# Query weights of a decode layer: eight loads of sixteen rows, eight partitions apart, in place of one load of 128 rows

## The chip, the cores and the metric

The kernel runs on one core of one Trainium2 chip. The metric is the device time of one execution in microseconds (us). One execution was also recorded by the hardware profiler; its lines are quoted as "the profile", and its events in order of time as "the trace". Engines are PE (TensorE matmul), PEld (its weight load), DVE (VectorE), ACT (ScalarE), POOL (GpSimd) and SP (SyncE, which here only issues DMAs); a name with q, such as SPq, is the sequencer of that engine.

## What is computed

One decode step of a transformer layer for a batch of 4, with a cache of 8192 positions for 32 heads of 128, in bf16:

```
h  = x + attention(layernorm(x), k_cache, v_cache, wq, wo)
       q = layernorm(x) @ wq                 # [4, 512] @ [512, 4096]
       p = softmax(q . k_cache / sqrt(128))  # for each batch and head
       o = (p . v_cache) @ wo                # [4, 4096] @ [4096, 512]
h2 = h + (sigmoid(n @ w_gate) * (n @ w_up)) @ w_down   # n = layernorm(h), 512 -> 1792 -> 512
```

## The kernel before

The 128 pairs of batch and head are worked in 32 units of four heads (NU = 32, HU = 4). The cache of a unit is 8 MB for K and 8 MB for V, and each is brought in by one DMA over 128 partitions, 64 KB a partition. The SBUF tile KV has three slots of that size: K goes to slots 0 and 1 in turn, V to slot 2 (the last V to slot 0). The weights borrow slots: the query weights wq (4 MB, 32 KB a partition) are in slot 2 at the start, before V0 takes it; wo, the gate and up weights follow the last K in slot 1, and the down weights follow in slot 2.

The program is a list of instructions for each engine, written out by the Python code with waits on semaphores (`prog.emit`, `prog.dma`); loops repeat two units at a time. No scheduler moves anything: each engine works in the order of its list.

SP's list holds all large loads on one queue. It begins with wq (L532), then the 64 cache loads (L541) in the order K0, K1, V0, K2, V1, K3, and so on, then wo, gate, up and down (L546 to L557). K0 and K1 wait for nothing. V0 waits for `t_qp`, the end of the q projection on PE, since it overwrites wq. A later K waits until DVE is through with the K two units before it (`t_kd`, L361), a later V until PE is through with the V one unit before it (`t_vd`, L419). A DMA raises its semaphore by 16 when it has landed; `t_wq = prog.token("wq", 16)` (L228) is the count that the readers of wq wait for.

The start on the other engines: the rows x are loaded by ACT's queue (L235), normalized by DVE and ACT (L273 to L277), turned by PE (L283). Then PE makes q in two groups of 16 matmuls (L301), which wait for wq, DVE turns the result (L308, L309) and builds the window Lq of the first query (L328). Per unit, DVE transposes K in chunks of 1024 words (L335), PE multiplies them (L344), DVE and ACT do the softmax (L362 to L375), PE multiplies with V (L405). After the last unit come the output projection (L475), a second layernorm and the gated feed-forward part (L501 to L530).

The destination and the source of the load that the diff touches:

```
reg(2, 0, NC * H * DH)                        # slot 2 of KV: 128 partitions x 16384 bf16
A_wq.rearrange("(p c) f -> p (c f)", p=128)   # 128 rows of 32 KB, contiguous in DRAM
```

Of the kernel before, what the change touches and what calls it, by code (L numbers as in the profile page):

```python
# [118 lines left out]
def bass_sequential_preLN__mha_block_cached__glu_gated_glu__decode_kernel(  # L119
# [13 lines left out]
    _, H, S, DH = A_k_cache.shape  # L133
    F = B_w_gate.shape[1]
    assert DH == 128 and H == 32 and D == 512 and F % 128 == 0 and B == 4 and S == 8192
    NC = D // 128
# [17 lines left out]
    prog = _Prog({"p2d": "dve", "d2d": "dve", "a2d": "dve", "d2p": "pe", "a2p": "pe",  # L154
                  "d2a": "act", "p2a": "act",
                  "k0": "dve", "k1": "dve", "v2": "pe"})
    emit = prog.emit

    with ExitStack() as es:
# [40 lines left out]
        def reg(slot, off, size):  # L200
            return KV[:, slot * SLOT + off:slot * SLOT + off + size]
# [23 lines left out]
        order = [("k", 0)] + [x for u in range(1, NU) for x in (("k", u), ("v", u - 1))] + [("v", NU - 1)]  # L225
        slots = {(x, u): (0 if u == NU - 1 else 2) if x == "v" else u % 2 for x, u in order}
        toks = {x: prog.token(x[0] + str(slots[x]), 16) for x in order}
        t_wq = prog.token("wq", 16)  # L228
        t_wo = prog.token("wo", 16)
        t_wg = prog.token("wg", 16)  # L230
        t_wu = [prog.token(f"wu{i}", 16) for i in range(len(WUC) - 1)]
# [293 lines left out]
        for t in range(NFT):  # L525
            if t == 0:
# [2 lines left out]
        t_o = [emit("dve", lambda e: e.tensor_copy(o_sb[:, 0:HD], bank[DN][0:B, 0:HD]), [t_d]),  # L529
               emit("act", lambda e: e.activation(o_sb[:, HD:D], bank[DN][32:32 + B, 0:HD], ACT.Copy), [t_d])]  # L530

        prog.dma("sp", "wq", lambda e: e.dma_start(reg(2, 0, NC * H * DH), A_wq.rearrange("(p c) f -> p (c f)", p=128)),  # L532
                 tok=t_wq)
        for n, (x, u) in enumerate(order):
            w = t_qp if n == 2 else None
            if n >= 3:
# [5 lines left out]
                     tok=toks[x, u])  # L542
# [49 lines left out]
```

## Time and profile before

| | |
|---|---|
| time, median of 3 runs | 1276.99 us (1276.86 to 1277.5) |
| the profiled execution, its time | 1276.65 us |
| its span in the profile | 1275.4 us |
| bytes read from DRAM | 550.77 MB, 432 GB/s over the span |
| mean granted TensorE clock | 0.823 |

The span runs from the first to the last recorded instruction; the time of the execution has 1.25 us around it. Three groups of instructions hold most of the busy time of the compute engines (columns: line, engine, operation, output and input tiles, shapes and count, then busy us and mean ns of one, then the idle time of the engine just before them and what ended most of it):

```profile
L335 DVE STREAM_TRANSPOSE kT<-KV 128x1024 f32<-128x1024 f32 x512 | 615.3, 1233 | 298.1 <-DMA KV<-in_A_k_cache_dram 237.2
L344 PE MATMUL PS<-kT,Lq 128*128 128x512 bf16 x2048 | 587.9, 419 | 315.5 <-DVE kT L335 298.5
L405 PE MATMUL PS<-KV,PTz 128*16 128x512 bf16 x2048 | 117.0, 381 | 0.3 <-DMA KV<-in_A_v_cache_dram 0.3
```

How to read it: a row of idle time names the releaser that ended it, here the K loads for DVE. A queue row of the DMA section gives packets, MB, and the time of its packets as a share of 16 engines' span. A row of DMA issues gives the median time from issue to landing, which includes what lay ahead in the queue.

### The profile page before, as it was taken

To read this page: it belongs to the slowest core of one execution; us is meant where nothing else is said; L and a number is where in the kernel's file an instruction comes from. 1 tells how busy PE (TensorE), PEld (TensorE's weight loads), DVE (VectorE), ACT (ScalarE), POOL (GpSimd) and SP (SyncE) were. 2 spreads that over 40 slices of the span, in tenths; PEclk is the share of its full clock that TensorE was granted. 3 is DMA by queue.
4 is the path that set the end of the run, shared out by engine and by line. 5 is a ranking of instruction groups with operands and counts; after the bars stand their busy time and mean duration, and the time that the engine had idled before them with its cause. 6 is when DMAs were issued, how large, how long until landed. Compare 5 with 4: busy or idle time off the path is not lost.

```text
span 1275.4 us, 14122 instructions
## 1 busy us (share of the span) xinstructions
PE 799.2 (63%) x4636; PEld 328.3 (26%) x4636; DVE 763.3 (60%) x917; ACT 58.9 (5%) x114; POOL 5.7 (0%) x22
## 2 busy tenths in 40 slices
PE   1676765557755557655567655567655576555677
PEld 0232222222222223222222222222222232222233
DVE  1876665556665557665567655566655566655571
ACT  2000000000000000000000000000000000000001
POOL 1000000000000000000000000000000000000000
PEclk9988877778877788777788877888777888777888
DMA  9999999999999999999999999999999999999998
GB/s 419 436 426 430 428 448 436 430 430 428 450 434 430 430 428 450 434 430 430 428 450 434 430 430 428 452 432 430 430 430 450 434 430 428 432 448 434 430 428 371
DMA packets 10388, 550.83 MB, mean 432 GB/s; under 512 B 1160, under 2 KB 1424, under 8 KB 1552
## 3 DMA queue, kind: packets, MB, share of 16 engines
q1 hardware_dynamic: 10368, 550.77, 99.7%
q8 instruction: 2, 0.03, 0.0%
q14 instruction: 2, 0.02, 0.0%
q10 hardware_dynamic: 16, 0.01, 0.0%
HBM read 550.77 MB, written 0.00 MB: 432 GB/s over the span
## 4 chain that ended last, share of the span: by engine, by line
DMA 41%; PE 13%; DVE 9%; issue 1%; ACT 1%; another core or an unknown queue 1%; SPq 0%; DVEq 0%
DMA KV<-in_A_k_cache_dram 39%; PE PS L344 10%; DVE kT L335 9%; PE PS L405 3%; DMA KV<-in_B_w_down_dram 3%; ACT kT L410 1%; PE PS L415 0%; SPq L541 0%; DVE PTz L375 0%; PE PS L521 0%; DVE KV L529 0%; SPq L557 0%; DVEq L112 0%
## 5 line engine op out<-in xcount | busy, mean ns | idle before, releaser
L335 DVE STREAM_TRANSPOSE kT<-KV 128x1024 f32<-128x1024 f32 x512 | 615.3, 1233 | 298.1 <-DMA KV<-in_A_k_cache_dram 237.2
L344 PE MATMUL PS<-kT,Lq 128*128 128x512 bf16 x2048 | 587.9, 419 | 315.5 <-DVE kT L335 298.5
L344 PEld LDWEIGHTS PS<-kT,Lq 128*128 x2048 | 210.1, 103 | 693.7 <-issue 620.7
L375 DVE STREAM_TRANSPOSE PTz<-E_sb 32x512 bf16<-32x512 bf16 x128 | 89.9, 703 | 129.1 <-PE PS L415 125.4
L405 PE MATMUL PS<-KV,PTz 128*16 128x512 bf16 x2048 | 117.0, 381 | 0.3 <-DMA KV<-in_A_v_cache_dram 0.3
L379 PE MATMUL PS<-part,headw 128*128 128x2 f32 x64 | 18.8, 363 | 100.5 <-DVE PTz L375 100.5
L369 ACT ACTIVATE E_sb<-PS,negm 128x512 bf16<-128x512 f32 x32 | 22.0, 687 | 1138.7 <-DVE negm L367 1138.7
L405 PEld LDWEIGHTS PS<-KV,PTz 128*16 128x16 bf16 x2048 | 58.8, 111 | 56.7 <-issue 13.2
L415 PE MATMUL PS<-lane,kT 128*128 128x4 f32 x256 | 33.6, 255 | 31.0 <-ACT kT L410 31.0
L362 DVE TENSOR_REDUCE part<-PS 128x1 f32<-128x512 f32 x32 | 22.1, 691 | 38.8 <-PE PS L344 38.8
L415 PEld LDWEIGHTS PS<-lane,kT 128*128 128x128 f32 x256 | 31.0, 191 | 46.2 <-issue 44.9
L379 PEld LDWEIGHTS PS<-part,headw 128*128 128x128 f32 x64 | 16.0, 310 | 103.7 <-DVE PTz L375 103.7
L322 PE MATMUL PS<-Lq,headw 128*128 128x512 bf16 x32 | 18.7, 585 | 10.8 <-issue 9.5
L410 ACT ACTIVATE kT<-PS,rsb 128x512 f32<-128x512 f32 x32 | 22.0, 687 | 61.2 <-PE PS L405 61.2
L388 PE MATMUL PS<-Lq 128*128 128x512 bf16 x44 | 13.2, 467 | 0.2 <-issue 0.2
L328 DVE TENSOR_TENSOR Lq<-q_all,mask 128x32 bf16<-128x32 bf16 x32 | 9.6, 300 | 0.0
L454 DVE TENSOR_TENSOR kT<-PS,mask 128x512 bf16<-128x512 f32 x1 | 0.7, 690 | 12.9 <-PE PS L415 12.9
L367 DVE STREAM_TRANSPOSE negm<-mxr 128x32 f32<-128x32 f32 x32 | 6.8, 212 | 1.1
L364 DVE STREAM_TRANSPOSE turn<-part 128x32 f32<-128x32 f32 x32 | 6.8, 212 | 1.1
L301 PE MATMUL PS<-KV,kT 128*4 128x512 bf16 x32 | 3.6, 627 | 5.4 <-DMA KV<-in_A_wq_dram 5.4
L388 PEld LDWEIGHTS PS<-Lq 128*128 128x128 bf16 x44 | 4.8, 115 | 8.1 <-issue 5.4
L396 DVE RECIPROCAL rsb<-PS 128x1 f32<-128x1 f32 x32 | 6.4, 199 | 0.7 <-PE PS L379 0.7
(70 smaller groups left out, 59.5 us busy)
## 6 DMA issues: line engine op xcount, KB each, us to landing
KV<-in_A_wq_dram SPq DMA_DIRECT2D x1, 4096.0 KB, 12.5
KV<-in_A_wo_dram SPq DMA_DIRECT2D x1, 4096.0 KB, 27.8
KV<-in_B_w_gate_dram SPq DMA_DIRECT2D x1, 1792.0 KB, 31.7
KV<-in_B_w_up_dram SPq DMA_DIRECT2D x1, 1792.0 KB, 35.5
KV<-in_B_w_down_dram SPq DMA_DIRECT2D x1, 1024.0 KB, 32.6
KV<-in_A_k_cache_dram SPq DMA_DIRECT2D x32, 49.6
KV<-in_A_v_cache_dram SPq DMA_DIRECT2D x32, 30.7
KV<-in_B_w_down_dram SPq DMA_DIRECT2D x1, 512.0 KB, 33.5
```

The costliest lines, as they stand in the source:

```text
L322: emit("pe", lambda e: e.matmul(bank[bk], headb, zeros, start=True, stop=False, skip_group_check=True), waits, incs=0)
L328: t_lq[u] = emit("dve", lambda e, ix: e.tensor_tensor(dst, bass.AP(raw(q_all), at(ix, 0) * (4 * TU) + 4 * (u - TU * t), [[NU * 4, 128], [1 ...
L335: t_tr[u, c] = emit("dve", lambda e: e.transpose(kT[:, (c % 2) * TW:(c % 2 + 1) * TW], KVw[:, o:o + TW]), w, ch="d2p")
L344: ins = e.matmul(bank[SBK], bass.AP(raw(Lq), ix[-1] * 2 + (128 * t + c % 2), [[528, 128], [1, 128]]), rhs, start=False, stop=False, skip_g ...
L362: a = emit("dve", lambda e: e.tensor_reduce(part[:, 0:1], bank[SBK], AX.X, ALU.max), [t_sc[u, NT - 1], t_pool], ch="d2d")
L369: t_exp[u] = emit("act", lambda e: e.activation(E_sb[:, :], bank[SBK], ACT.Exp, bias=negm[:, 0:1], scale=SCALE, accum_out=part[:, 1:2]), [ ...
L375: return [e.transpose(PTz[32 * q:32 * (q + 1), :].rearrange("p (r q c) -> p r q c", r=4, q=4)[:, :, q, :], E_sb[32 * q:32 * (q + 1), :].re ...
L379: t_sum[u] = emit("pe", lambda e: e.matmul(bank[QB[1]][:, 0:2], headw[:, :], part[:, 0:2], start=True, stop=True), [t_ptz[u], t_selc], ch= ...
L388: emit("pe", lambda e: [e.matmul(bank[XS], Lq[:, 0:128], Lq[:, 0:512], start=True, stop=True) for _ in range(n)][-1], [t_ps0, t_lq[NU - 1] ...
L405: made.append(e.matmul(PS[32 * j:32 * j + 16, ob:ob + 512], lhsT, KV[:, slot * SLOT + 512 * k:slot * SLOT + 512 * (k + 1)], start=(k < 4), ...
L410: t_ocp[u] = emit("act", lambda e: e.activation(O_sb, bank[OBK], ACT.Copy, scale=rsb[:, 0:1]), [t_pv[u], t_rs[u]], ch="a2p")
L415: ins = e.matmul(bass.AP(raw(PS), at(ix, 0) * 4 + (512 * EX + 4 * (u - t)), [[4096, 128], [1, 4]]), O_sb[:, 128 * q:128 * (q + 1)], lane[: ...
```

## The change

The one load of wq becomes eight. Load r takes rows r, r + 8, r + 16, ..., r + 120 of the source into the same partitions of slot 2, so that sixteen rows of 32 KB move with each load; together the eight write the same bytes to the same places. All eight raise the same semaphore, and `t_wq` is its count after all of them. They are issued one after the other from SP's list, ahead of K0.

```
-        t_wq = prog.token("wq", 16)
+        t_wq = prog.token("wq", 8 * 16)
...
-        prog.dma("sp", "wq", lambda e: e.dma_start(reg(2, 0, NC * H * DH), A_wq.rearrange("(p c) f -> p (c f)", p=128)),
-                 tok=t_wq)
+        wq_src = A_wq.rearrange("(p c) f -> p (c f)", p=128)
+        for r in range(8):
+            prog.dma("sp", "wq", lambda e, r=r: e.dma_start(reg(2, 0, NC * H * DH)[r:128:8, :], wq_src[r:128:8, :]), tok=t_wq)
```

SP's list at the start of the program, before (each row: line, what is issued, tiles and shape, repetitions, semaphores waited for; s_pe is the end of the q projection, s_d2x that of a K, s_p2x that of a V):

```order
L532 DMA KV<-in_A_wq_dram 128x16384 [waits barrier_Pool_Activation_PE_DVE_SP_release]
L541 DMA KV<-in_A_k_cache_dram 128x32768 x2
L541 DMA KV<-in_A_v_cache_dram 128x32768 [waits s_pe]
L541 DMA KV<-in_A_k_cache_dram 128x32768 [waits s_d2x]
L541 DMA KV<-in_A_v_cache_dram 128x32768 [waits s_p2x]
```

One load of 128 rows precedes K0 there. SP's list at the same place after the change:

```order
L534 DMA KV<-in_A_wq_dram 16x16384 [waits barrier_Pool_Activation_PE_DVE_SP_release]
L534 DMA KV<-in_A_wq_dram 16x16384 x7
L542 DMA KV<-in_A_k_cache_dram 128x32768 x2
L542 DMA KV<-in_A_v_cache_dram 128x32768 [waits s_pe]
L542 DMA KV<-in_A_k_cache_dram 128x32768 [waits s_d2x]
L542 DMA KV<-in_A_v_cache_dram 128x32768 [waits s_p2x]
```

Seven loads more stand ahead of K0, and all that follows has moved down by seven places, with the same waits.

PE's list at the q projection, which is the same before and after (the line numbers too):

```order
L283 MATMUL PS<-ident,kT 128x4 [waits s_dve]
L283 MATMUL PS<-ident,kT 128x4 x3
L301 MATMUL PS<-KV,kT 4x512 [waits s_act,s_pool,s_dve,s_wq]
L301 MATMUL PS<-KV,kT 4x512 x31
L433 MATMUL PS<-PTz 128x128 [waits s_pool]
L322 MATMUL PS<-Lq,headw 128x512 [waits s_d2p]
```

The first matmul of L301 is the only place that waits for wq; the count it waits for is 16 before and 128 after. No instruction of PE, DVE, ACT or POOL is added or moved.

## The prediction

> **What bounds the kernel now.** I read the page first (busy shares, the row of the DMA engines, the chain that ended last), then the windows, to see whether the transfers ever pause, then the timeline of the first 33 us, where the edit lies. The page:
>
> ```profile
> span 1275.4 us, 14122 instructions
> PE 799.2 (63%) x4636; PEld 328.3 (26%) x4636; DVE 763.3 (60%) x917; ACT 58.9 (5%) x114; POOL 5.7 (0%) x22
> DMA packets 10388, 550.83 MB, mean 432 GB/s; under 512 B 1160, under 2 KB 1424, under 8 KB 1552
> q1 hardware_dynamic: 10368, 550.77, 99.7%
> q10 hardware_dynamic: 16, 0.01, 0.0%
> DMA 41%; PE 13%; DVE 9%; issue 1%; ACT 1%; another core or an unknown queue 1%; SPq 0%; DVEq 0%
> ```
>
> No compute engine is busy for more than 63% of the span, while the packets of SP's queue (q1) fill 99.7% of the time of the 16 DMA engines. The chain names compute at many steps because a load waits for the buffer that compute frees; what counts is whether the engines ever ran dry in such a wait. The windows answer that (columns: stretch, its length, busy time and count of each engine, granted TensorE clock, DMA share, GB/s):
>
> ```profile
> 13.40:32.70 19.30, 4.41 (x34) 1.13 (x34) 2.03 (x5) 0.00 (x0) 0.00 (x0) 1.00 1.00 435
> 52.10:129.60 77.50, 51.44 (x291) 21.15 (x289) 53.39 (x69) 3.71 (x8) 0.00 (x0) 0.85 1.00 432
> 207.00:1175.00 968.00, 605.07 (x3476) 249.65 (x3477) 590.81 (x702) 36.62 (x75) 0.00 (x0) 0.81 1.00 434
> 1252.00:1271.50 19.50, 15.19 (x150) 5.99 (x139) 4.28 (x11) 5.57 (x9) 0.00 (x0) 0.91 0.98 415
> ```
>
> The share is 1.00 at 432 to 435 GB/s in three windows from the landing of the query weights to 1175 us, and still 0.98 among the last weights, with granted clocks between 0.81 and 1.00. So the kernel is one unbroken stream of transfers, 27.1 GB/s for each of 16 engines (434 / 16), and the compute follows it. Time added to the stream anywhere adds to the span; time saved shortens it. How far ahead the queue is filled:
>
> ```profile
> KV<-in_A_wq_dram SPq DMA_DIRECT2D x1, 4096.0 KB, 12.5
> KV<-in_A_k_cache_dram SPq DMA_DIRECT2D x32, 49.6
> KV<-in_A_v_cache_dram SPq DMA_DIRECT2D x32, 30.7
> ```
>
> An 8 MB cache load needs 19.3 us at 435 GB/s, and lands 49.6 us (K) or 30.7 us (V) after its issue: at the median 30 or 11 us of other transfers lie ahead of it. The start of the program, from the timeline:
>
> ```profile
> 0.80 0.38 SPq L532 DMA_DIRECT2D KV<-in_A_wq_dram  x1
> 1.24 0.89 SPq L541 DMA_DIRECT2D KV<-in_A_k_cache_dram  x2
> 13.39 3.59 PE L301 MATMUL PS<-KV,kT 128*4 128x512 bf16 x32 [5.44 <-DMA KV<-in_A_wq_dram]
> 17.10 0.33 SPq L541 DMA_DIRECT2D KV<-in_A_v_cache_dram  x1
> 18.16 0.29 DVE L328 TENSOR_TENSOR Lq<-q_all,mask 128x32 bf16<-128x32 bf16 x1
> 32.66 2.37 DVE L335 STREAM_TRANSPOSE kT<-KV 128x1024 f32<-128x1024 f32 x2 [14.21 <-DMA KV<-in_A_k_cache_dram]
> ```
>
> The query weights land at 13.39 us, the window of the first query is done at 18.45 us, and DVE then waits 14.21 us for K0. The computation of q is therefore not on the path; the bytes of the weights are, since K0, K1 and all later loads stand behind them.
>
> **The change, part by part.**
>
> *Descriptors.* q1 has 10368 packets for 72 loads, 144 each: 128 rows and 16 completion records (72 x 16 = 1152 of the 1160 packets under 512 B). The two ACT transfers of 4 rows make the 16 packets of q10, 8 each: 4 rows and 4 completions, so four engines. A load of 16 rows then has one row and one completion on each of 16 engines, and eight loads have 128 rows and 128 completions, 112 more records than before. Cost: the stream at share 1.00 in the middle window holds 50 loads' completions (968 / 19.36) without a gap that the share shows, so I take 0 us; the bound is 0.5% of one 9.6 us load, 0.05 us, times seven, 0.4 us.
>
> *Issue.* The nearest row for several loads issued back to back is the down projection at the end:
>
> ```profile
> 1238.73 1.75 SPq L557 DMA_DIRECT2D KV<-in_B_w_down_dram  x4
> ```
>
> 0.44 us each. Eight take 3.5 us, in place of 0.38 and a gap of 0.06: K0 and K1 are issued at 4.3 and 4.8 us, not 1.24 and 1.7, and SP's wait for V0 begins at 5.2. What hides this is the transfer itself: one 16-row load is 0.52 MB, 1.2 us at 435 GB/s, and the next arrives after 0.44 us. The queue stays filled and K0 is in it long before the weights end. Cost 0; if a load took over 1.2 us to issue, the cover would be gone, and the excess counted eight times.
>
> *Start.* 4.19 MB take 9.64 us at the rate of K0 (half of 32.66 - 13.39 = 19.27 us, K0's own time), but the weights need 12.5 us from issue to landing. The other 2.9 us are start-up. The first load of 16 rows could begin a little sooner than one of 128. I take nothing; 2.9 us is the most that could be gained.
>
> *The wait on the weights.* One semaphore, now at 128 in place of 16, so the first matmul of L301 still waits for all eight loads; nothing starts early. Behind it on PE are the 32 matmuls of q and the clear of L322; V0 waits for them (issued at 17.10), and V0 has until K1 ends, 13.39 + 2 x 19.3 = 52.0 us. That cover is 35 us. If the weights come 9.6 us later, K1 ends 9.6 us later too, and the cover stays.
>
> *Which rows are written at once.* This is the term that decides. Before, all loads of this kernel's SP queue cover 128 partitions, and each engine has eight of them. After, at any moment the 16 engines write 16 rows eight partitions apart. The rate is the same within 1% whether K alone moves (435 GB/s, first window) or K and V in turn (432 and 434), under any load of the compute engines, so I put the limit not in the source but in the engine or in its way into SBUF. If it is in the engine, nothing changes: 0 us. If it is in the way, it matters to which ways the sixteen rows belong. Were a way eight consecutive partitions, each of the sixteen rows would have its own: 0 us. [...]
>
> [...]
>
> **The sum.** Against the profiled execution, 1276.65 us (1275.4 us of span and 1.25 us around it): descriptors 0, issue 0, start 0, wait 0, rows 9.6, thus 1286.25; this execution lies 0.34 us below the median of the runs before (1276.99), well inside 0.2%. I forecast **1286.3 us**, 0.7% slower.
>
> **The rivals.**
>
> 1. *No sharing.* The limit is in the engine, or the ways are eights. The weights still land near 13.4 us, and the time is 1276.7, from 1276.65 - 0.5 to + 0.5. For it: no load in the trace shows sharing, and a 16-row load has all 16 engines by the count above. Against it: nothing but that no row shows full rate into 16 partitions at a time. This ends on the other side of the forecast. [...]
>
> [...]
>
> 3. *Each load pays a start-up.* If the 2.9 us between 12.5 and 9.64 us were paid by each of eight loads, seven more cost 20 us: 1297. Against it: the 50 loads of the middle window pay nothing of the kind, at share 1.00; they have eight rows an engine behind which a completion can hide, and the new ones have one. [...]
>
> 4. *A quicker start.* Up to the 2.9 us above, without sharing: 1273.8 at best.
>
> **How the numbers follow.** Forecast 0.60. No sharing 0.23: the rows leave it open, and I put it well behind since it needs one of two special arrangements. Sharing that undoes itself 0.11. Start-up per load 0.03. Quicker start 0.03. A measurement of this kernel tells about 0.2%, 2.6 us, from no change. So slower is 0.60 + 0.11 + 0.03 = 0.74, the same 0.23, faster 0.03. Forecast and undone sharing hold only 0.71, so the range reaches to no sharing, with its 0.5 us below: 1276.2. Upwards it goes to the forecast's own end: 9.6 us, 0.4 for the records and 1.4 if half of the start-up's 2.9 us is paid once more, 1288.1. The forecast's own range is 1285 to 1288.1, its lower end for a start that is quicker by 1.3.
>
> **What would show it.** [...] K0 must land 19.3 us after the weights in every case, and the middle window stay at 434 GB/s; DVE's wait for K0 should stay at about 14.2 us, as both of its ends move. SP's eight issues should end near 4.3 us. The prediction is wrong if the weights land before 20 us, or if they land late and the end is not late by the same amount, which would mean slack in the stream that the share of 1.00 denies.

## The result, and the profile after

| | before | after |
|---|---|---|
| time, median (lowest to highest) | 1276.92 us (1276.72 to 1277.5), 6 runs | 1287.71 us (1287.18 to 1288.25), 6 runs |
| the profiled execution: time, span | 1276.65, 1275.4 us | 1288.25, 1287.0 us |

The kernel became slower: ratio 1.0084, 95% interval 1.0074 to 1.0094, 10.8 us by the medians. The profiled execution after is the slowest of its six, so its span lies 11.6 us above that of before; the medians carry the size, the profile the place. In the experiments below one execution of e7_halves took 1444.65 us at a granted clock of 0.79, where the others had 0.82; its median counts it, its ratio does not.

The page after (busy shares, packets, queue, chain of waits):

```profile
span 1287.0 us, 14129 instructions
PE 801.0 (62%) x4636; PEld 328.4 (26%) x4636; DVE 763.2 (59%) x917; ACT 58.9 (5%) x114; POOL 5.7 (0%) x22
GB/s 261 456 424 424 438 440 426 432 444 426 426 446 432 426 442 436 426 442 436 426 440 438 426 434 444 426 434 444 426 432 446 426 426 452 426 424 450 430 424 367
DMA packets 10500, 550.83 MB, mean 428 GB/s; under 512 B 1272, under 2 KB 1536, under 8 KB 1664
q1 hardware_dynamic: 10480, 550.77, 99.7%
DMA 60%; PE 19%; DVE 12%; issue 2%; ACT 1%; SPq 0%; DVEq 0%
```

The bytes are the same and the queue's packets still fill 99.7% of 16 engines' span, with 112 packets more. But the first slice of 32 us carries 261 GB/s, where it carried 419 before:

```profile
GB/s 419 436 426 430 428 448 436 430 430 428 450 434 430 430 428 450 434 430 430 428 450 434 430 430 428 452 432 430 430 430 450 434 430 428 432 448 434 430 428 371
```

The other slices are much as they were: 424 to 456 and 367 in the last, before 426 to 452 and 371. The engines were not idle in the first; their packets took longer, 2.56 us a row from the second round on (2.33 in the fifth), where it was 1.21. The opening on the timeline:

```profile
0.80 5.03 SPq L534 DMA_DIRECT2D KV<-in_A_wq_dram  x8
5.87 1.05 SPq L542 DMA_DIRECT2D KV<-in_A_k_cache_dram  x2
23.73 3.59 PE L301 MATMUL PS<-KV,kT 128*4 128x512 bf16 x32 [15.78 <-DMA KV<-in_A_wq_dram]
27.43 0.33 SPq L542 DMA_DIRECT2D KV<-in_A_v_cache_dram  x1
42.85 2.37 DVE L335 STREAM_TRANSPOSE kT<-KV 128x1024 f32<-128x1024 f32 x2 [14.07 <-DMA KV<-in_A_k_cache_dram]
```

The weights land at 23.73 us (13.39 before, +10.34), K0 at 42.85 (32.66 before, +10.19), and DVE waits as long for K0 as it did. The rate behind it, in windows after (columns as in the windows of the prediction):

```profile
4.00:12.00 8.00, 0.29 (x4) 0.21 (x4) 0.74 (x3) 4.22 (x6) 3.32 (x6) 1.00 1.02 209
24.50:43.80 19.30, 3.65 (x30) 0.90 (x22) 2.94 (x5) 0.00 (x0) 0.00 (x0) 1.00 1.00 435
218.00:1186.00 968.00, 606.18 (x3476) 249.73 (x3477) 591.19 (x702) 36.62 (x75) 0.00 (x0) 0.81 1.00 434
```

And the first of these windows before the change:

```profile
4.00:12.00 8.00, 0.29 (x4) 0.21 (x4) 0.74 (x3) 4.22 (x6) 3.32 (x6) 1.00 0.97 418
```

From 4 to 12 us the kernel before moves 418 GB/s and the changed one 209, each at a DMA share of about 1: half the rate at full occupancy. From K0 on both stream at 434 to 435.

### The profile page after: what moved, and what is told of

Same layout as the page of the kernel before. It is cut to its first block, busy times and chain, and to the rows that moved or that the text cites. A ratio compares the mean times of both kernels' runs of the same rounds, so it can differ in the third digit from the quotient of the medians.

```text
span 1287.0 us, 14129 instructions
## 1 busy us (share of the span) xinstructions
PE 801.0 (62%) x4636; PEld 328.4 (26%) x4636; DVE 763.2 (59%) x917; ACT 58.9 (5%) x114; POOL 5.7 (0%) x22
## 3 DMA queue, kind: packets, MB, share of 16 engines
q1 hardware_dynamic: 10480, 550.77, 99.7%
## 4 chain that ended last, share of the span: by engine, by line
DMA 60%; PE 19%; DVE 12%; issue 2%; ACT 1%; SPq 0%; DVEq 0%
DMA KV<-in_A_k_cache_dram 57%; PE PS L344 14%; DVE kT L335 12%; PE PS L405 5%; DMA KV<-in_B_w_down_dram 3%; ACT kT L410 1%; PE PS L415 0%; SPq L542 0%; DVE PTz L375 0%; PE PS L521 0%; DVE KV L529 0%; SPq L558 0%; DVEq L112 0%
## 5 line engine op out<-in xcount | busy, mean ns | idle before, releaser
L362 DVE TENSOR_REDUCE part<-PS 128x1 f32<-128x512 f32 x32 | 22.1, 692 | 38.7 <-PE PS L344 38.7
L322 PE MATMUL PS<-Lq,headw 128*128 128x512 bf16 x32 | 18.8, 586 | 10.8 <-issue 9.5
L301 PE MATMUL PS<-KV,kT 128*4 128x512 bf16 x32 | 3.6, 627 | 15.8 <-DMA KV<-in_A_wq_dram 15.8
```

What stands on the lines that cost most here:

```text
L322: emit("pe", lambda e: e.matmul(bank[bk], headb, zeros, start=True, stop=False, skip_group_check=True), waits, incs=0)
L362: a = emit("dve", lambda e: e.tensor_reduce(part[:, 0:1], bank[SBK], AX.X, ALU.max), [t_sc[u, NT - 1], t_pool], ch="d2d")
```

## The experiments

Three theories were to be told apart. **Shared ways**: with some choices of partitions, engines that write at the same time share one way into SBUF and each gets a part of its rate; this is the author's assumption, and the runs show the rate of each choice, not which partitions would belong to one way. **Count**: eight loads cost more than one, whatever they cover. **Source**: rows 256 KB apart in DRAM are read slowly. Each edit below replaces the load of wq in the kernel before, unless it says otherwise; `dst` is slot 2 as 128 partitions x 16384 and `wq_src` the source as 128 rows; where the number of loads is another, the count of `t_wq` follows it. The ratios are taken over the executions of a kernel and are not ratios of the medians.

### Eight loads, all partitions in each (e1_columns)

```
+        for r in range(8):
+            prog.dma("sp", "wq", ... reg(2, 2048 * r, 2048), wq_src[:, 2048 * r:2048 * (r + 1)] ..., tok=t_wq)
```

> Eight loads again, but each covers all 128 partitions and one eighth of the columns (4 KB a row, 0.52 MB a load). Shared ways (two engines write through one way into SBUF when sixteen rows eight partitions apart move at once): nothing is shared, the weights land at 13.4 to 14 us and the time is 1276.9, at most 1278 for the slower issue. Count of loads (each of eight loads, with its completions and its issue, costs something): as the change, about 1287.7, weights near 23.7 us. Source rows 256 KB apart: not present here, 1276.9.

Measured: 1277.63 us against 1276.98, ratio 1.0008 (0.9999 to 1.0018), single executions from 1276.46 to 1279.89. The timeline of this run's opening:

```profile
0.80 3.83 SPq L534 DMA_DIRECT2D KV<-in_A_wq_dram  x8
13.37 3.58 PE L301 MATMUL PS<-KV,kT 128*4 128x512 bf16 x32 [5.42 <-DMA KV<-in_A_wq_dram]
```

Eight loads with eight issues and 128 completions land at 13.37 us, as one load does (13.39). The count is not the cause.

### Destination eight apart, source in one piece (e2_source)

```
+            prog.dma("sp", "wq", ... dst[r:128:8, :], wq_src[16 * r:16 * (r + 1), :] ..., tok=t_wq)
```

> Destination as in the change (sixteen partitions eight apart), source sixteen consecutive rows of 32 KB, 512 KB in one piece; the rows of wq thus come to other partitions than they belong to. Shared ways: as the change, 1287.7 (1287 to 1288.5), weights at 23.5 to 24 us. Source (rows 256 KB apart read slowly): back to 1277 or 1278. Count of loads: 1287.7, which this run does not tell from shared ways.

Measured: 1286.73 us against 1276.98, ratio 1.0099 (1.0065 to 1.0134): 9.8 us by the medians, a little under the expected 1287 to 1288.5. Three of the four executions lie at 1286.64 to 1286.73; the fourth took 1295.25, which raises the ratio and widens its interval. The timeline and one window of this run:

```profile
23.49 3.44 PE L301 MATMUL PS<-KV,kT 128*4 128x512 bf16 x32 [15.54 <-DMA KV<-in_A_wq_dram]
```

```profile
4.00:12.00 8.00, 0.29 (x4) 0.21 (x4) 0.74 (x3) 4.22 (x6) 3.32 (x6) 1.00 1.01 209
```

With the source in pieces of 512 KB the price stays, at the same 209 GB/s. The distance of the source rows is not the cause. What is left is the destination, which the next run changes alone.

### Sixteen consecutive partitions (e3_consecutive)

```
+            prog.dma("sp", "wq", ... dst[16 * r:16 * (r + 1), :], wq_src[16 * r:16 * (r + 1), :] ..., tok=t_wq)
```

> Eight loads of sixteen consecutive partitions, source rows consecutive too; same count, same bytes as the change. [...] Count of loads: 1287.7. Source: 1277 to 1278. Ways of eight consecutive partitions (which the change has already spoken against): two ways, 1276.9 + 68 = 1345.

Measured: 1302.74 us against 1276.98, ratio 1.0201 (1.0184 to 1.0218): 25.8 us more, and none of the times named above. Timeline and window of this run:

```profile
0.80 3.64 SPq L534 DMA_DIRECT2D KV<-in_A_wq_dram  x8
39.59 3.59 PE L301 MATMUL PS<-KV,kT 128*4 128x512 bf16 x32 [31.64 <-DMA KV<-in_A_wq_dram]
```

```profile
4.00:36.00 32.00, 0.29 (x4) 0.21 (x4) 0.72 (x3) 4.23 (x6) 3.32 (x6) 1.00 1.02 115
```

About a quarter of the full rate: 115 GB/s against 435, a row of 4.61 us (median, from the packet records) against 1.21. Were a way eight consecutive partitions, it would have been an eighth. The eight loads read the same source rows as those of e2_source, in the same pieces; the choice of partitions alone took the time from 1286.73 to 1302.74 us, 16.0 more.

### The same split on another weight (e4_wo)

The query weights come whole, and the output weights wo, late in a filled queue, in eight loads:

```
-        prog.dma("sp", "wo", ... reg(1, 0, WOJ * D), A_wo.rearrange("(p j) f -> p (j f)", p=128) ..., [k_done], tok=t_wo)
+        for r in range(8):
+            prog.dma("sp", "wo", ... reg(1, 0, WOJ * D)[r:128:8, :], wo_src[r:128:8, :] ..., [k_done], tok=t_wo)
```

> The query weights come in one load again; the output weights wo (4 MB, 128 rows of 32 KB) come in eight loads of sixteen rows eight apart, in the middle of a filled queue near the end. Shared ways: the same price at another place, +10 to +11, 1287 to 1288, with rows of about 2.56 us. A cost of the program's start (an empty queue, or start-up paid eight times): 1277 to 1279. Count of loads: 1287 to 1288 as well.

Measured: 1288.57 us against 1276.98, ratio 1.0093 (1.0076 to 1.011). Two windows of this run, in the stream of the caches and while wo moves:

```profile
1200.00:1248.00 48.00, 27.99 (x153) 12.84 (x160) 26.30 (x33) 2.15 (x4) 0.00 (x0) 0.80 1.01 436
1252.00:1266.00 14.00, 7.90 (x82) 4.13 (x86) 0.98 (x2) 2.17 (x3) 0.00 (x0) 0.88 0.93 193
```

The price is paid there too, 11.6 us, slightly over the expected 10 to 11. From the second round on, wo's rows took 2.29 to 2.56 us by the packet records (medians of sixteen), where they took 1.21 before. The price does not belong to the start of the program.

### The loads in alternating order (e5_alternate)

```
-        for r in range(8):
+        for r in (0, 4, 1, 5, 2, 6, 3, 7):
```

> The eight loads of the change in the order r = 0, 4, 1, 5, 2, 6, 3, 7. In the change the rows of the fifth round, the first with r over 3, took 2.33 us and all other rounds 2.56: two engines that share a way do not start together, and where both move on to another way the first has it alone for a moment. Shared ways with such a lead: each of seven switches saves about 0.23 us and not one, so rounds of 2.33 us from the second on, weights at 22.1 to 22.6 us, time 1286.0 to 1286.6. Shared ways without it: as the change, 1287.7, weights at 23.5 us. If the leads grew until two engines took turns: down to 1282. Count of loads or source: 1287.7.

Measured: 1285.97 us against 1276.75, ratio 1.0074 (1.0057 to 1.0091), weights at 22.74 us, a little later than the expected 22.1 to 22.6:

```profile
22.74 3.25 PE L301 MATMUL PS<-KV,kT 128*4 128x512 bf16 x32 [14.78 <-DMA KV<-in_A_wq_dram]
```

The packets of the 128 rows, in the order of their starts, make eight rounds of sixteen; where a load has 16 rows, it is one round. The medians of how long a row's packet took, in us, from the packet records of the traces (e7_halves and e8_step2 are for the sections on them):

```
round              1     2     3     4     5     6     7     8
before           1.86  1.21  1.21  1.21  1.21  1.21  1.21  1.21
after            2.16  2.56  2.56  2.56  2.33  2.56  2.56  2.56
e5_alternate     2.26  2.39  2.37  2.37  2.38  2.37  2.37  2.37
e3_consecutive   3.67  4.58  4.60  4.61  4.62  4.61  4.61  4.62
e7_halves        2.11  2.57  2.57  2.55  2.38  2.57  2.57  2.56
e8_step2         2.18  2.56  2.56  2.56  2.36  2.56  2.56  2.56
```

From the second on every round is shorter now, 2.37 to 2.39 us, by 0.17 to 0.19 us (0.23 expected), where after the change only the fifth is. So the time of a round depends on the order of the loads too, with the same rows in each. That one engine has a way alone for a moment is the author's explanation; which engine takes which row is not in the records. The engines never came to take turns: the rounds stay at 2.37 to 2.39.

### Four loads of 32 rows, four apart (e6_rows32)

```
+        for r in range(4):
+            prog.dma("sp", "wq", ... dst[r:128:4, :], wq_src[r:128:4, :] ..., tok=t_wq)
```

> [...] If a load deals neighbouring rows to an engine, two to each, engine e writes partition 8e + r and then 8e + 4 + r, so that at any moment two engines still share a way and a switch comes after each row: as the alternating order, 1285.5 to 1287. If rows are dealt so that an engine stays in one way, as the single load of 128 rows must do to reach 27 GB/s an engine: 1276.9 to 1278, weights near 13.5 us. Only the number of loads: about half of the change's price, 1282.

Measured: 1277.27 us against 1276.75, ratio 1.0005 (0.9995 to 1.0014). Timeline and window of this run:

```profile
13.37 3.20 PE L301 MATMUL PS<-KV,kT 128*4 128x512 bf16 x32 [5.42 <-DMA KV<-in_A_wq_dram]
```

```profile
4.00:12.00 8.00, 0.29 (x4) 0.21 (x4) 0.74 (x3) 4.22 (x6) 3.32 (x6) 1.00 1.07 459
```

No price at all (a window of 8 us counts whole packets, hence 459). Rows took 1.21 us (medians of the packet records from the third round on), as in the load of 128 rows. By the theory of shared ways a load of 32 rows would then be dealt so that no two engines meet, which the records do not show. The number of loads again costs nothing.

### Two halves of 64 partitions (e7_halves)

```
+        for r in range(2):
+            prog.dma("sp", "wq", ... dst[64 * r:64 * (r + 1), :], wq_src[64 * r:64 * (r + 1), :] ..., tok=t_wq)
```

> Two loads of 64 rows, partitions 0 to 63 and 64 to 127. [...] Number of loads: under 1279.

Measured: 1287.67 us against 1276.75, ratio 1.0083 (1.0062 to 1.0103). Timeline and window of this run:

```profile
23.72 3.59 PE L301 MATMUL PS<-KV,kT 128*4 128x512 bf16 x32 [15.77 <-DMA KV<-in_A_wq_dram]
```

```profile
4.00:12.00 8.00, 0.29 (x4) 0.21 (x4) 0.74 (x3) 4.22 (x6) 3.32 (x6) 1.00 0.98 201
```

Two loads of 2 MB, with contiguous source and neighbouring partitions, cost what the change costs, 10.9 us by the medians. With rows of 2.57 us at a share of 0.98 the engines are all at work, at 201 GB/s. Neither the distance between the partitions nor the number of loads is needed for the price: two loads into neighbours pay it as eight with gaps do.

### Sixteen rows, two apart (e8_step2)

```
+        for j in range(4):
+            for r in range(2):
+                prog.dma("sp", "wq", ... dst[32 * j + r:32 * j + 32:2, :], wq_src[32 * j + r:32 * j + 32:2, :] ..., tok=t_wq)
```

> Eight loads of sixteen rows two partitions apart: partitions 32 j to 32 j + 31, even ones, then odd ones. [...] No sharing: 1277 to 1278.

Measured: 1287.44 us against 1277.14, ratio 1.0106 (1.0066 to 1.0147), rows of 2.56 us (table above). Three of the four executions lie at 1286.93 to 1287.89 us, one at 1297.45, which raises the ratio as in e2. The weights:

```profile
23.88 3.59 PE L301 MATMUL PS<-KV,kT 128*4 128x512 bf16 x32 [15.93 <-DMA KV<-in_A_wq_dram]
```

Sixteen rows spread over 32 partitions cost what sixteen spread over all 128 cost, 2.56 us a row, and less than sixteen neighbours, 4.61 (e3). No sharing (1277 to 1278) is excluded. In e7 and in this run the fifth round alone is short (2.38 and 2.36 us), where the loads go over to partitions 64 and up; after the change it is the fifth as well (2.33), there the first with r over 3. Which partitions slow each other is not shown beyond these choices.

### Two loads of 64 rows, two apart (e9_rows64)

```
+        for r in range(2):
+            prog.dma("sp", "wq", ... dst[r:128:2, :], wq_src[r:128:2, :] ..., tok=t_wq)
```

> [...] If rows are dealt so that an engine stays in one way, as with 32 rows four apart: 1276.9 to 1278, weights near 13.4 us. If a load's rows are dealt as neighbours, four to an engine: two engines share a way at any moment, 1286 to 1288.

Measured: 1276.97 us against 1277.14, ratio 1.0 (0.9991 to 1.001). The timeline of this run:

```profile
0.80 1.19 SPq L534 DMA_DIRECT2D KV<-in_A_wq_dram  x2
13.34 3.59 PE L301 MATMUL PS<-KV,kT 128*4 128x512 bf16 x32 [5.39 <-DMA KV<-in_A_wq_dram]
```

Same number of loads and of rows as the halves, other partitions: 10.7 us apart. No run beats the kernel before; e1, e6 and e9 equal it within their intervals, since the stream is full in all of them (419, 459 and 459 GB/s from 4 to 12 us).

## Why the prediction was right

*The bound.* Right: one unbroken stream. What the weights lost at the start (K0 +10.19 us) arrived at the end (+10.8 by medians), and the middle window moved 434 GB/s as before.

*Which rows are written at once.* Right in direction, and the term was a little small: 9.6 us forecast, 10.3 measured at the weights (13.39 to 23.73 us). No run shows what the 9.6 us of the sum rest on, two engines to one way; the runs showed rows of 2.56 us in place of 1.21 for sixteen rows eight partitions apart, and 209 GB/s in place of 418. By the packet records the first row starts 0.40 us later and takes 0.30 longer; then come six rounds of 2.56 in place of 1.21 and one of 2.33, 6 x 1.35 + 1.12 = 9.2 us. That is 9.9 us to the end of the last packet, and the matmul that waits begins 0.4 us later still after it, 10.3 in all. The forecast amounts to eight rounds of twice 1.21: the rounds of 2.56 are 6% longer than that, and the first round, 1.86 us before and 2.16 after, is not doubled (why was not tested). So the seven later rounds cost 9.2 us and not seven times 1.21, which is 8.5; the first cost 0.7 and not 1.2; and the 0.4 behind the last packet had no term. It goes with the longer rows: the matmul begins 0.3 to 0.4 us after the last packet before and in e1, e6 and e9, 0.7 to 1.1 us after it in the change, e2, e5, e7 and e8, and 1.5 in e3; why is open.

The uncertainty named in this term, a limit in the engine or in its way into SBUF, is settled as far as the engine goes by e2, e3, e7 and e9: the engines busy throughout (shares of 0.98 to 1.06), the same bytes, other partitions, another rate. The prediction's reason against the source, that K alone and K and V in turn move at one rate, did not tell source and engine apart; e2 and e3 did. No row of before had a load into a part of the partitions at this length; the change, e3 and e6 to e9 measured the rates, and how the partitions are arranged in ways stays unshown. The time lies in the upper part of the forecast's own range, which was left for the records (0.4, and e1 shows no such cost) and for half a start-up paid once more (1.4).

*Descriptors.* Right: the 112 further records were counted, and e1 with as many completions lands at 13.37 us, as one load does (13.39).

*Issue.* Wrong in size, and the stream did not wait for it: eight issues took 5.03 us, 0.63 each, not 0.44 from the row of the down projection. The cover of 1.2 us a round held, and it was 2.56.

*Start.* Not quicker; the first row began 0.4 us later. This is not the slower rows: in e6 and e9, whose weights land as early as before, it begins 0.34 us later too, and in e3, whose rows are the slowest, at 1.82 us, when it did before. It goes with the length of the first issue (0.56 us or more there, 0.38 in e3 and before); why, and whether it costs anything, is open, since the weights of e9 land no later than before.

*The wait.* Right: V0 was issued at 27.43 us, 10.3 later, and K1's last packet ended 10.1 later.

*The rivals.* No sharing is excluded by the landing at 23.73 us, which it had near 13.4, and start-up per load by e1, which lands at 13.37 us with eight loads. Sharing that undoes itself would need rows at full rate; after the change no round has a median under 2.16 us, against 1.21. The order of the loads does matter, but it is worth 0.2 us a round (e5), not a row. A quicker start is excluded by the first row, 0.40 us later.

*What stays open.* Which partitions slow each other, beyond the choices measured; why a row then takes 2.56 us and not 2.42, twice 1.21; and the 0.6 us between K0's shift and that of the median end. The latter differs from execution to execution: in the trace of e2 K0 is late by 9.88 us and the span by 10.1, in that of e7 by 10.28 and 10.7, in the profiled execution of the change by 10.19 and 11.6. Part of it is not the change's own: by the packet records the sixth cache load ends 10.5 us later after the change, K0 10.1, and in e6 and e9, whose K0 ends when it did before, the sixth ends 0.6 and 0.4 us later as well.

## What to carry to other kernels

Where the stream of transfers is the bound, look at which partitions are written at the same moment, not at the number of loads. Loads of 128 partitions, of 64 two apart (e9) and of 32 four apart (e6) had the weights there at 13.34 to 13.39 us. Of 64 neighbours (e7), sixteen eight apart (the change) and sixteen two apart (e8) a row took 2.56 to 2.57 us in most rounds in place of 1.21, and of sixteen neighbours (e3) 4.61. A DMA share near 1 does not say that the engines move at full rate (1.02 at 209 GB/s after the change, 0.97 at 418 before, from 4 to 12 us); read the GB/s beside it. Splitting a load along its columns was free here (e1); splitting it along partitions cost between nothing (e6, e9) and 2% (e3). All of this is for rows of 32 KB (4 KB in e1) on one queue.

## What the runs showed of the hardware that was not expected

The time that SP needed to issue a load went with its shape, but not with the number of rows alone. Eight loads of sixteen rows took 5.03 us eight partitions apart and 3.64 with the partitions consecutive (e3); eight with all 128 rows and a part of the columns took 3.83 (e1); two of 64 rows took 1.20 consecutive (e7) and 1.19 two apart (e9). What decides is not shown.

The slower rows are not whole multiples of the 1.21 us of before, and the step differs. Two rows in 2.56 us are 25.6 GB/s (2 x 32768 B), less than the 27.1 of one row in 1.21. In e3 a row took 4.61 us and not the 5.12 that twice 2.56 would be; how much of that comes from the order of the rows, as in e5, was not tested.
